# A second level of Strassen's algorithm for the first two weight products of eight token blocks, with weight forms kept in HBM

## The chip, the cores and the metric

The kernel runs on one core of a Trainium2 chip. Its engines are TensorE (PE, with its weight loads shown apart as PEld), VectorE (DVE), ScalarE (ACT), GpSimd (POOL) and SyncE (SP), which issues DMAs; ACT issues some DMAs too. The metric is device time in microseconds of one execution, as the median of several.

## The reference

```python
# attention, float32: 8 batches, 8 heads, 576 positions, head size 64
scores = (1.0 / np.sqrt(64)) * np.matmul(q, k.transpose(0, 1, 3, 2))
gamma = 1.0 - 2.0 ** (-5.0 - np.arange(8))
Dmat = np.where(rel >= 0, gamma[:, None, None] ** rel[None], 0.0)   # rel = i - j
attn_out = np.matmul(scores * Dmat[None], v)
# feed forward over 8*576 = 4608 tokens of width 512
x = attn_out.transpose(0, 2, 1, 3).reshape(4608, 512)
a = x @ w1            # 512 -> 1024
b = x @ w2            # 512 -> 1024
out = ((a * b) @ w3) @ w_out     # 1024 -> 1024 -> 512
```

q, k and v come as float32, the four weights as float64.

## The kernel before

**Start.** The weights are read as float64 and converted to float32 on the chip. w3 and w_out are multiplied with each other once (`w3_mm`, L499) into `w3o`, 1024x512, so that each token afterwards needs only two products: `x` with w1 and w2, and `a*b` with `w3o`. This is mixed with the first pair of batches.

**Attention.** Batches are taken in four pairs. The 576 positions of a pair are cut into five chunks of 64, 128, 128, 128 and 128 positions, which gives 20 chunk steps `g`. In one step `pv(g)` multiplies masked scores with v and the running state (L296, L321) and ACT copies the result into `xT` (L328), token columns of x; then `state(g + 1)` (L277) and `score(g + 1)` (L255) run for the next chunk. From chunk 7 on (`in_blocks`), q and k are brought in by `load_blocks` (L182, DMAs at L193): 32 DMAs of 32 KB on SP's queue for a chunk of 128 positions, 16 for one of 64, into two buffers of the tag `ld_q`, one for q and one for k. DVE transposes them out of these buffers (`front_blocks`, L212), after POOL has scaled q (`scale_blocks`, L203). POOL also scales v (L226). v, and k in token order, are loaded on ACT's queue.

**Feed forward.** The tokens of a pair are cut into three blocks of 192 positions by two batches, twelve blocks `m` in all. `up(i, n, fp)` (L529) computes one quarter of the columns of a and b for one block by Strassen's algorithm: the depth is halved, and the two batches of the block are the two columns of the token matrix. It has seven products of four matmuls of 128x128 by 128x192 (L546), a float32 matmul standing as two records in the trace. The weight operands are prepared once, in place, in two tiles `wA` (A11, A12, S3, A22) and two tiles `wS` (S1, S2, S4), one of each per half of the 1024 columns (`strassen_weights`, L171). The token operands of a block are prepared by POOL (`strassen_tokens`, L518). ACT and DVE move the products out of PSUM: ACT copies at L559 and L574, DVE adds at L551 (`plus`), and DVE multiplies the a part with the b part into `ab` at the end (L580). PSUM's pool `acc` holds seven buffers.

`down` (L645) takes two tiles of 128 tokens of `ab` and multiplies them with `w3o` (L661), again by Strassen: seven products of four matmuls by 128x256, added by DVE (L665) into the tile `ot`, which has one buffer, and stored on ACT's queue (L709). Its token operands (L627, L631, L633) are formed by DVE beforehand: `ahead` puts them on the list `aside`, from which each `plus` of an `up` takes one. `carry` (L611) copies the third tile of tokens of an even block away, so that it can be paired with that of the next block.

**Order.** All engines run in the order in which the program issues to them. `todo` lists the calls of `up`, `carry` and `down` that are ready, and `work(n)` does the next `n` of them. In chunk step `g` the order is: n - 1 pieces of work; one more piece, among whose additions DVE's two transposes for chunk g + 1 are put (through `aside`); the loads of chunk g + 2 on SP (`load_blocks`); then `pv(g)`, loads of v and k on ACT's queue, `state` and `score` of g + 1, and the scaling on POOL. `n` is the length of `todo` divided by the chunk steps left in the pair. After the last chunk of a pair `add_pair` adds the pair's work to `todo`.

Of the kernel before, what the change touches and what calls it, by code (L numbers as in the profile page):

```python
# [12 lines left out]
BF16 = mybir.dt.bfloat16  # L13
ALU = mybir.AluOpType
PSUM = bass.MemoryType.PSUM

@with_exitstack
def kernel(
# [13 lines left out]
    nc = tc.nc  # L57
# [448 lines left out]
    def has_x(i, n):  # L506
        return any(starts[c] + sizes[c] >= (n + 1) * TB and ("x", i * NC + c) in live for c in range(NC))
# [21 lines left out]
    def up(i, n, fp, conv=0, tail=True, first=False):  # L529
        m = every.index((i, n))  # L530
        while ("S", fp) not in live:
            assert go_on() is None
        if ("B", i, n) not in live:
            list(strassen_tokens(i, n))
        if fp == 0:
            live["ab", i, n] = (pools["ab3"] if m == 2 else ffn).tile([P, 2 * KF, TB], F32, tag="ab", name="ab")
        ab = live["ab", i, n]

        def product(ps, a, b):
            a, b = A(fp, a), live["B", i, n][b]  # L540
            new = ps is None
            if new:
                ps = acc.tile([P, 2, TB], F32, tag="acc", name="up")
            for w in range(2):
                for r in range(2):
                    nc.tensor.matmul(ps[:, w, :], a[:, w, r, :], b[:, r, :], start=(new and w == r == 0),  # L546
                                     stop=(w == r == 1), skip_group_check=True)
            return ps

        def plus(ps, to, sb):  # L550
            nc.vector.tensor_add(c[:, to], ps, c[:, sb])  # L551
            convert(conv.pop(0) if isinstance(conv, list) else conv)
            if aside:
                aside.pop(0)()


        c = ffn.tile([P, 4, 2, TB], F32, tag="c", name="c", bufs=1)
        p1 = product(None, "A11", "B11")
        nc.scalar.copy(c[:, 0], p1)  # L559

        convert(owed.pop() if owed else 0)
        if first:

            p7 = product(None, "S3", "T3")
            product(p1, "A12", "B21")
            aside.pop(0)()
        plus(product(None, "S2", "T2"), 1, 0)
        plus(p7 if first else product(None, "S3", "T3"), 2, 1)
        p5 = product(None, "S1", "T1")
        plus(p5, 3, 2)  # L570
        plus(product(None, "A22", "-T4"), 2, 2)
        if not first:
            product(p1, "A12", "B21")
        nc.scalar.copy(c[:, 0], p1)  # L574
        product(p5, "S4", "B22")
        plus(p5, 1, 1)

        if fp == NQ - 1 and m + 1 < len(every) and has_x(*every[m + 1]) and ("B", *every[m + 1]) not in live:
            list(strassen_tokens(*every[m + 1]))
        nc.vector.tensor_mul(ab[:, 4 * fp:4 * fp + 4, :], c[:, :, 0, :], c[:, :, 1, :])  # L580
        if tail:
            convert(conv)

    aside, owed = [], []

    def w3_sums():

# [53 lines left out]
            aside.append(todo_sums.pop(0))  # L643

    def down(x, y, then=None, last=False):  # L645
        for m, t in (x, y):
            if t == 2 and m % 2 == 0 and m > 0:
                assert (m, t) in carried
        a, done, left = pair_of(x, y)
        ahead(x, y)  # L650
        while len(done) < 3:
# [11 lines left out]

        def plus(nm, to, sb):
            nc.vector.tensor_add(ot[:, to[0], to[1]], ps[nm], ot[:, sb[0], sb[1]])  # L665

        def put(m, t, row, half=slice(0, 2)):

# [176 lines left out]
    load_blocks(NC + 1, "q")  # L845
    keep_stores.clear()
    store()
    todo = [(down, (0, 0), (0, 1)), (down, (1, 0), (1, 1)), (down, (0, 2), (1, 2))]

    def add_pair(i):  # L850

        for n in range(NB):
            m = every.index((i, n))
            if m != NB:
                todo.append((up, i, n, 1))
            if m > NB and m % 2 == 0:
                todo.append((down, (m - 2, 2), (m - 1, 2)))
            if m != NB:
                todo.extend((up, i, n, fp) for fp in range(2, NQ))
            if m + 1 < len(every):  # L860
                todo.append((up, *every[m + 1], 0))
                if m % 2 == 0:
                    todo.append((carry, m, 2))
            else:
                todo.append((down, (m - 1, 2), (m, 2)))
            todo.append((down, (m, 0), (m, 1)))

    def work(n):
        for _ in range(min(n, len(todo))):
            fn, *args = todo.pop(0)  # L870

            nxt = next((x for x in todo if x[0] is not carry), None)
            if nxt and nxt[0] is down and fn is not carry:
                if fn is down:
                    args.append(nxt[1:])
                else:
                    last = args == [*every[max(nxt[1][0], nxt[2][0])], NQ - 1]
                    ahead(*nxt[1:], 1 if last else 3)
            if g == G and not todo:
                fn(*args, last=True)  # L880
            else:
                fn(*args)

    g = NC
    scale_blocks(NC)
# [4 lines left out]
    score(NC)  # L890
    scale_blocks(NC + 1)
    in_blocks = [u >= 2 * NC - 3 for u in range(G)] + [False] * 2
    for g in range(NC, G):
        c = g % NC

        n = (1, 1, 2, 2, 1)[c] if g < 2 * NC else -(-len(todo) // (NC - c))
        if g + 2 < G and not in_blocks[g + 2]:
            load(g + 2, "k")
            load_blocks(g + 2, "q")
        if g + 1 < G:  # L900
            scale(g + 1, "v")
            if not in_blocks[g + 1]:
                front(g + 1, "k")
                front_blocks(g + 1, "q")
        half = (n + 1) // 2
        if in_blocks[g + 1]:
            scale_blocks(g + 1)

            work(n - 1)
            aside.extend(lambda nm=nm: front_blocks(g + 1, nm) for nm in "kq")  # L910
            work(1)
            while aside:
                aside.pop(0)()
            half = 0
        if in_blocks[g + 2]:
            load_blocks(g + 2, "q")
            load_blocks(g + 2, "k")
        work(half)
        pv(g)()

        if g + 2 < G:
            queue = nc.scalar if in_blocks[g + 2] else nc.sync
            load(g + 2, "v", queue)
            if in_blocks[g + 2] and (g + 2) % NC != NC - 1:
                load(g + 2, "k", queue)
        if g + 1 < G:
            state(g + 1)
            score(g + 1)
        if g + 2 < G and not in_blocks[g + 2]:
            scale_blocks(g + 2)  # L930
        if g == NC + 1:
            list(strassen_tokens(1, 0))
            todo.extend((up, 1, 0, fp) for fp in range(NQ))
        if not (in_blocks[g + 1] and g + 1 < G):
            work(n // 2)
        if c == NC - 1:
            add_pair(g // NC)
    g = G
    work(len(todo))

# [42 lines left out]
```

## Time and profile before

| what | value |
|---|---|
| runs | 856.2, 856.49 and 858.15 us |
| median | 856.49 us |
| span of the profiled execution | 853.3 us |
| mean granted TensorE clock in it | 0.996 |
| moved by DMA | 64.52 MB, 76 GB/s over the span |
| ACT copies of an `up` (128x384) | 479 ns at L559, 476 at L574 |
| DVE multiplication at the end of an `up` (128x768) | 983 ns |
| POOL scaling of v (128x1024) | 1963 ns |

The span is what the profiler saw from the first to the last instruction; the runs are timed apart, and their median is 3.2 us above it. The profile's busy time of an engine is a sum over instructions, so an engine that is busy 98% of the span has few gaps, while one that is busy 55% may still be the last to arrive at some place. A group line gives the program line, the engine, the operation, the tile written and those read, the shape, the count, the busy time and mean duration, and then the idle time of the engine ahead of these instructions with what ended it. A name with q (SPq) is the time for which an engine's instruction queue was held at that place, by issuing or by waiting.

### The profile page before, as it was taken

The numbers are of one execution on the slowest core, as the hardware profiler recorded it, in microseconds if no ns is written. First come the engines' busy times: TensorE is split into PE (matmuls) and PEld (weight loads), VectorE is DVE, ScalarE is ACT, GpSimd is POOL, SyncE is SP. The second block draws the span as 40 slices with busy tenths as digits, with TensorE's granted clock in tenths as the row PEclk, the third lists the DMA queues.
The fourth block names the chain that finished last, engine by engine and source line by source line (L and its number), as shares of the span: only waits on it lengthen the run. The fifth ranks groups of instructions, "written<-read, shape, count | busy, mean of one in ns | idle before, by whom it ended". The sixth has DMA issues, their size and how long they took to land.

```text
span 853.3 us, 15401 instructions
## 1 busy us (share of the span) xinstructions
PE 839.5 (98%) x6273; PEld 766.0 (90%) x6273; DVE 469.8 (55%) x763; ACT 205.7 (24%) x385; POOL 111.0 (13%) x95
## 2 busy tenths in 40 slices
PE   7999999999999999999999999999999999999998
PEld 6889999644888999999999999999999999999996
DVE  4999999990744454454545444544454434334343
ACT  4777566670111102011111010110100201001000
POOL 1100010002104113130230130203030101000000
PEclk8999999999999999999999999999999999999999
DMA  9994554526057446252452161542130000000001
GB/s 193 223 228 113 77 151 121 142 80 111 12 107 122 83 69 107 53 101 45 79 97 46 24 108 36 90 82 43 38 62 26 2 25 1 25 26 1 25 1 49
DMA packets 220485, 64.52 MB, mean 76 GB/s; under 512 B 201336, under 2 KB 211832, under 8 KB 220416
## 3 DMA queue, kind: packets, MB, share of 16 engines
q1 hardware_dynamic: 169856, 42.80, 26.1%
q10 hardware_dynamic: 50560, 20.75, 10.9%
q8 instruction: 49, 0.80, 0.4%
q14 instruction: 20, 0.16, 0.1%
HBM read 54.08 MB, written 9.44 MB: 74 GB/s over the span
## 4 chain that ended last, share of the span: by engine, by line
PE 88%; DVE 6%; DMA 3%; issue 2%; ACT 1%; SPq 0%; POOL 0%; ACTq 0%; DVEq 0%; POOLq 0%
PE up L546 46%; PE po L661 25%; PE ps L499 6%; PE xps L321 4%; PE sc L255 4%; DMA ld_v<-in_v_dram 2%; PE xps L296 2%; PE st L277 2%; DVE c L551 1%; DVE m L424 1%; PE tp L240 1%; DVE wS L171 1%; DVE e L435 1%; DMA out_dram<-ot 1%; DMA raw<-in_moe_w_out_dram 0%
## 5 line engine op out<-in xcount | busy, mean ns | idle before, releaser
L551 DVE TENSOR_TENSOR c<-up,c 128x384 f32<-128x384 f32 x240 | 132.5, 552 | 180.0 <-PE up L546 176.2
L546 PE MATMUL up<-xT,wA 128*128 128x192 f32 x1152 | 212.0, 327 | 0.0
L546 PEld LDWEIGHTS up<-xT,wA 128*128 128x128 f32 x1152 | 190.6, 190 | 2.8 <-issue 0.5
L546 PE MATMUL up<-T,wS 128*128 128x192 f32 x768 | 140.4, 326 | 0.9 <-DVE wS L171 0.9
L546 PEld LDWEIGHTS up<-T,wS 128*128 128x128 f32 x768 | 127.4, 190 | 1.1 <-ACT c L559 1.1
L661 PE MATMUL po<-w3o,ab 128*128 128x256 f32 x456 | 104.3, 380 | 0.6 <-DVE ab L627 0.3
L661 PEld LDWEIGHTS po<-w3o,ab 128*128 128x128 f32 x456 | 85.9, 190 | 12.8 <-DVE ab L627 0.7
L665 DVE TENSOR_TENSOR ot<-po,ot 128x256 f32<-128x256 f32 x90 | 38.1, 423 | 71.6 <-PE po L661 68.3
L574 ACT COPY c<-up 128x384 f32<-128x384 f32 x48 | 22.9, 476 | 218.8 <-PE up L546 212.8
L226 POOL TENSOR_TENSOR ld_v<-ld_v,gk 128x1024 f32<-128x1024 f32 (+1 forms) x18 | 35.3, 1963 | 298.9 <-DMA ld_v<-in_v_dram 214.5
L546 PE MATMUL up<-xT,wS 128*128 128x192 f32 x384 | 70.9, 328 | 1.6 <-DVE c L551 1.6
L546 PE MATMUL up<-T,wA 128*128 128x192 f32 x384 | 70.2, 326 | 0.0
L258 DVE TENSOR_TENSOR pm<-sc,mask 128x512 f32<-128x512 f32 (+1 forms) x80 | 45.4, 628 | 41.0 <-PE sc L255 41.0
L546 PEld LDWEIGHTS up<-xT,wS 128*128 128x128 f32 x384 | 63.4, 190 | 2.9 <-DVE c L551 2.7
L661 PE MATMUL po<-wB,forms 128*128 128x256 f32 x288 | 65.1, 379 | 0.0
L546 PEld LDWEIGHTS up<-T,wA 128*128 128x128 f32 x384 | 63.7, 190 | 0.0
L661 PEld LDWEIGHTS po<-wB,forms 128*128 128x128 f32 x288 | 54.7, 190 | 7.4
L499 PE MATMUL ps<-wo,w3T 128*128 128x512 f32 x128 | 55.1, 592 | 0.0
L559 ACT COPY c<-up 128x384 f32<-128x384 f32 x48 | 23.0, 479 | 132.1 <-PE up L546 77.4
L499 PEld LDWEIGHTS ps<-wo,w3T 128*128 128x128 f32 x128 | 24.3, 190 | 30.1 <-issue 29.7
L580 DVE TENSOR_TENSOR ab<-c 128x768 f32<-128x768 f32 x48 | 47.2, 983 | 4.3 <-ACT c L574 0.6
L203 POOL TENSOR_TENSOR bl_q<-bl_q,gqs 128x512 f32<-128x512 f32 (+1 forms) x30 | 32.4, 1100 | 100.3 <-DMA bl_q<-in_q_dram 92.5
(80 smaller groups left out, 797.6 us busy)
## 6 DMA issues: line engine op xcount, KB each, us to landing
raw<-in_moe_w_dram SPq DMA_DIRECT2D x72, 128.0 KB, 3.0
bl_q<-in_q_dram SPq DMA_DIRECT2D x216, 32.0 KB, 2.2
bl_k<-in_k_dram SPq DMA_DIRECT2D x192, 32.0 KB, 2.1
out_dram<-ot ACTq DMA_DIRECT2D x23, 256.0 KB, 2.0
ld_v<-in_v_dram ACTq DMA_DIRECT2D x11, 512.0 KB, 5.9
raw<-in_moe_w_dram SPq DMA_DIRECT2D x16, 256.0 KB, 6.2
raw<-in_moe_w_out_dram SPq DMA_DIRECT2D x32, 128.0 KB, 2.8
ld_k<-in_k_dram ACTq DMA_DIRECT2D x8, 512.0 KB, 8.3
```

The costliest lines, as they stand in the source:

```text
L203: nc.gpsimd.tensor_tensor(out=part, in0=part, in1=gqs[:, :, n0:n0 + n].unsqueeze(3).to_broadcast([P, NP, n, BL]), op=ALU.mult)
L226: engine.tensor_tensor(out=t, in0=t, in1=gam[:sz, c].unsqueeze(1).unsqueeze(3).to_broadcast([sz, 2, H, D]), op=ALU.mult)
L255: nc.tensor.matmul(sc[j][:sz, p, :sz], kT[hs, b, p, :sz], qT[hs, b, p, :sz], start=True, stop=True)
L258: nc.vector.tensor_mul(pm[:sz, b, j, :, :sz], sc[j][:sz, :, :sz], mask[:sz, :sz].unsqueeze(1).to_broadcast([sz, NP, sz]))
L321: nc.tensor.matmul(banks[r][heads[half], b, n, :sz], vs[:sz, b * H + 2 * p + j, :], pm[:sz, b, j, p, :sz], start=(c == 0 and m == 0), stop ...
L499: nc.tensor.matmul(ps, live["w3T", ft][:, g, :], live["wo"][:, g, :], start=(g == 0), stop=(g == KF - 1))
L546: nc.tensor.matmul(ps[:, w, :], a[:, w, r, :], b[:, r, :], start=(new and w == r == 0), stop=(w == r == 1), skip_group_check=True)
L551: nc.vector.tensor_add(c[:, to], ps, c[:, sb])
L559: nc.scalar.copy(c[:, 0], p1)
L580: nc.vector.tensor_mul(ab[:, 4 * fp:4 * fp + 4, :], c[:, :, 0, :], c[:, :, 1, :])
L661: nc.tensor.matmul(ps[nm], a[A][:, f, :], live["W"][B][:, f, :], start=(f == 0 and not on), stop=(f == NP - 1), skip_group_check=True)
L665: nc.vector.tensor_add(ot[:, to[0], to[1]], ps[nm], ot[:, sb[0], sb[1]])
```

## The change

Blocks 0 to 3 are computed as before. Blocks 4 to 11 are taken in four groups of two, and `up` is replaced there by `up2`, which applies Strassen's algorithm twice. The two blocks of a group are the two token columns of the outer level; the inner level is the former one.

**Steps.** For a group and a half of the 1024 columns the outer level has seven operands (P1, P2, P6, P7, P4, P5, P3 in this order), and each is one step, a call of `up2`: seven products of two matmuls by 128x192 each. There are 4 groups x 2 halves x 7 = 56 steps in place of 8 x 4 = 32 calls of `up`. The results of the steps are added among each other by POOL (`combine`, on tiles of 128x768 elements), from four tiles `cc`, and DVE multiplies a with b for each finished quarter (`multiply`).

**Weight forms.** Each half has seven outer operands, each with seven inner ones. They are computed on DVE in place (`weight_forms`), by two sets of additions per half, and each set is followed by DMAs on SP (14 per set, 28 per half) that store what it has finished in HBM tiles `kept`. One operand is 128 x 1792 elements, 917,504 bytes. These pieces are put on a list `spread`, from which `plus` of `up` and `plus` of `down` take one each. Afterwards `wA` is used again as a ring of three slots for operands read back (`open_second`), and `wS` as the `cc` tiles. `next_forms` issues the read of one operand on SP, in the step after the slot's last use, for the step two later.

**Token forms.** `token_forms` makes both levels of token operands for a group by 19 operations on POOL, at the end of the chunk step in which the group's tokens are complete.

**Order.** `n` comes from a written list, `dealt`. The downs of a group follow its 14 steps, one after the other. In the last chunk step all `n` pieces come ahead of `pv`. `carry` is used for block 2 alone. The down (1, 0), (1, 1) and that of (2, 2), (3, 2) move behind the `up`s of block 3 = (1, 0), in whose additions the weight forms are computed.

```diff
             convert(conv.pop(0) if isinstance(conv, list) else conv)
-            if aside:
-                aside.pop(0)()
+            for extra in (aside, spread):
+                if extra:
+                    extra.pop(0)()
...
-    todo = [(down, (0, 0), (0, 1)), (down, (1, 0), (1, 1)), (down, (0, 2), (1, 2))]
-
-    def add_pair(i):
-
-        for n in range(NB):
-            m = every.index((i, n))
-            if m != NB:
-                todo.append((up, i, n, 1))
-            if m > NB and m % 2 == 0:
-                todo.append((down, (m - 2, 2), (m - 1, 2)))
-            if m != NB:
-                todo.extend((up, i, n, fp) for fp in range(2, NQ))
-            if m + 1 < len(every):
-                todo.append((up, *every[m + 1], 0))
-                if m % 2 == 0:
-                    todo.append((carry, m, 2))
-            else:
-                todo.append((down, (m - 1, 2), (m, 2)))
-            todo.append((down, (m, 0), (m, 1)))
+    todo = [(down, (0, 0), (0, 1)), (down, (0, 2), (1, 2))]
...
+    FORM = 14 * P
+    OPERANDS = {"P1": ("A11", "B11"), "P2": ("A12", "B21"), "P6": ("S2", "T2"), "P7": ("S3", "T3"),
+                "P4": ("A22", "-T4"), "P5": ("S1", "T1"), "P3": ("S4", "B22")}
+    PLACE = {"A11": (0, 0), "A12": (1, 0), "S3": (0, 1), "A22": (1, 1)}
+    hbm = ctx.enter_context(tc.tile_pool(name="hbm", bufs=1, space=DRAM))
+    kept = {(h, nm): hbm.tile([P, FORM], F32, tag=f"kept{h}{nm}", name="kept")
+            for h in halves for nm in (*PLACE, "S1", "S2", "S4")}
...
+    def weight_forms(h, second):
+
+        wa, ws = wA[h].rearrange("p r j c n -> p (r j) c n"), wS[h]
+
+        def tt(out, in0, in1, op):
+            def both():
+                for w in (wa, ws):
+                    o, x, y = (w[:, :, c, m * QC:(m + 1) * QC] if w is wa else w[:, :, m, :, c, :]
+                               for m, c in (out, in0, in1))
+                    nc.vector.tensor_tensor(out=o, in0=x, in1=y, op=op)
+            return both
+
+        def send(pieces):
+            for nm in (*PLACE, "S1", "S2", "S4"):
+                to = kept[h, nm]
+                for lo, m, c in pieces:
+                    n = 2 * P if c == 1 else 4 * P
+                    d = to[:, lo:lo + n].rearrange("p (g n) -> p g n", n=P)
+                    cs = slice(0, 2) if c is None else slice(c, c + 1)
+                    if nm in PLACE:
+                        r, f = PLACE[nm]
+                        x = wA[h][:, r, :, cs, m * QC + f * P:m * QC + f * P + P]
+                    else:
+                        x = wS[h][:, ("S1", "S2", "S4").index(nm), m, :, cs, :]
+                    nc.sync.dma_start(d.rearrange("p (j c) n -> p j c n", j=2), x)
+
+        if second:
+            return [tt((1, 1), (1, 1), (1, 0), ALU.subtract), tt((0, 0), (1, 1), (0, 0), ALU.add),
+                    tt((0, 1), (0, 1), (1, 1), ALU.subtract),
+                    lambda: send([(8 * P, 0, None), (12 * P, 1, 1)])]
+        return [tt((1, 0), (0, 0), (1, 0), ALU.subtract), lambda: send([(0, 0, None), (4 * P, 1, None)])]
...
+    order = ("P1", "P2", "P6", "P7", "P4", "P5", "P3")
+    ring, sent, steps, free = [], [0], [0], []
+    groups = [(m, m + 1) for m in range(4, len(every), 2)]
...
+    def open_second():
+        while spread:
+            spread.pop(0)()
+        ra = [wp.tile([P, 32 * P], F32, tag=f"wA{h}", name="ra") for h in halves]
+        cs = [wp.tile([P, 2, 4, 2, TB], F32, tag=f"wS{h}", name="cc") for h in halves]
+        ring.extend([ra[0][:, :FORM], ra[0][:, FORM:2 * FORM], ra[1][:, :FORM]])
+        free.extend(cs[h][:, j] for h in halves for j in range(2))
+        live["T2"] = ra[1][:, FORM:].rearrange("p (s k c t) -> p s k c t", s=2, k=3, c=2)
...
+        for _ in range(2):
+            next_forms()
+        live["U"] = [ffn.tile([P, 2, TB], F32, tag="T", name="u", bufs=5) for _ in range(5)]
...
+    def next_forms():
+        n = sent[0]
+        if n < 14 * len(groups):
+            nc.sync.dma_start(ring[n % 3], kept[n % 14 // 7, OPERANDS[order[n % 7]][0]])
+            sent[0] += 1
...
+    def multiply():
+        while results:
+            gr, h, f, b, z, used = results.pop(0)
+            for s, m in enumerate(groups[gr]):
+                if ("ab", *every[m]) not in live:
+                    live["ab", *every[m]] = ffn.tile([P, 2 * KF, TB], F32, tag="ab", name="ab")
+                ab = live["ab", *every[m]].rearrange("p (q i) t -> p q i t", i=4)[:, 2 * h:2 * h + 2, 2 * f + b, :]
+                v = z.rearrange("p (m s) w t -> p m s w t", s=2)[:, :, s]
+                nc.vector.tensor_mul(ab, v[:, :, 0, :], v[:, :, 1, :])
+            free.append(z)
...
+    def up2(gr, n):
+
+        h, key = n // 7, order[n % 7]
+        slot = ring[steps[0] % 3]
+        B = live["B2", gr][OPERANDS[key][1]]
+        steps[0] += 1
+        c = free.pop(0)
+        sums2[key] = c
...
+        adds = {"P1": [], "P2": [("P2", "P1")], "P6": [("P6", "P1")], "P7": [("P7", "P6")], "P4": [("P4", "P7")],
+                "P5": [("P7", "P5"), ("P6", "P5")], "P3": [("P3", "P6")]}[key]
...
+            for w in range(2):
+                nc.tensor.matmul(ps[:, w, :], weight_of(slot, a, w), B[b], start=(new and w == 0), stop=True,
+                                 skip_group_check=True)
...
+        def combine(part):
+            for into, of in adds:
+                o, i = sums2[into][:, part], sums2[of][:, part]
+                nc.gpsimd.tensor_tensor(out=o, in0=o, in1=i, op=ALU.add)
+
+        p1 = product(None, "A11", "B11")
+        nc.scalar.copy(c[:, 0], p1)
+        finish()
+        next_forms()
+        plus(product(None, "S2", "T2"), 1, 0)
+        plus(product(None, "S3", "T3"), 2, 1)
+        p5 = product(None, "S1", "T1")
+        plus(p5, 3, 2)
+        plus(product(None, "A22", "-T4"), 2, 2)
+        combine(slice(2, 4))
+        multiply()
+        product(p1, "A12", "B21")
+        nc.scalar.copy(c[:, 0], p1)
+
+        def rest():
+            product(p5, "S4", "B22")
+            plus(p5, 1, 1)
...
+    real = (up, up2, down)
+
+    def add_group(gr):
+        X, Y = groups[gr]
+        todo.extend((up2, gr, n) for n in range(14))
+        todo.extend([(close_up2,), (down, (X, 0), (X, 1)), (down, (X, 2), (Y, 2)), (down, (Y, 0), (Y, 1))])
...
-            nxt = next((x for x in todo if x[0] is not carry), None)
-            if nxt and nxt[0] is down and fn is not carry:
+            nxt = next((x for x in todo if x[0] in real), None)
+            if nxt and nxt[0] is down:
                 if fn is down:
                     args.append(nxt[1:])
                 else:
-                    last = args == [*every[max(nxt[1][0], nxt[2][0])], NQ - 1]
-                    ahead(*nxt[1:], 1 if last else 3)
+                    ahead(*nxt[1:], 1 if fn is up2 else 3)
             if g == G and not todo:
                 fn(*args, last=True)
             else:
                 fn(*args)
+            n -= 1
+            while todo and todo[0][0] not in real:
+                todo.pop(0)[0]()
...
+    dealt = [1, 1, 2, 2, 2, 3, 4, 4, 4, 3, 7, 7, 3, 7, 7]
     for g in range(NC, G):
         c = g % NC
-
-        n = (1, 1, 2, 2, 1)[c] if g < 2 * NC else -(-len(todo) // (NC - c))
+        n = dealt[g - NC]
...
+            forms = [(lambda h=h, second=second: spread.extend(weight_forms(h, second)),)
+                     for h in halves for second in (False, True)]
+            ups = [(up, 1, 0, fp) for fp in range(NQ)]
+            todo.extend([*ups[:2], forms[0], ups[2], forms[1], ups[3], forms[2], (down, (1, 0), (1, 1)), forms[3],
+                         (down, (2, 2), (3, 2)), (open_second,), (down, (3, 0), (3, 1))])
...
+        if not (in_blocks[g + 1] and g + 1 < G) and half:
             work(n // 2)
-        if c == NC - 1:
-            add_pair(g // NC)
+        if g == 2 * NC - 1:
+            add_group(0)
+        ready = {2 * NC - 1: 0, 2 * NC + 3: 1, 3 * NC + 1: 2, G - 1: 3}
+        if g in ready:
+            token_forms(ready[g])
+            if ready[g]:
+                add_group(ready[g])
```

The other functions are `open_second`'s further tiles, the body of `token_forms` (additions and subtractions on POOL between views of `xT`, `T2`, `E` and `U`), and `weight_of`, which picks one 128x128 weight tile out of a slot.

## The prediction

> **What bounds the kernel now.** I read the page's busy table and slices, then the chain of waits in order of time, then the SP queue's timeline, since the change puts 56 large loads there.
>
> ```profile
> PE 839.5 (98%) x6273; PEld 766.0 (90%) x6273; DVE 469.8 (55%) x763; ACT 205.7 (24%) x385; POOL 111.0 (13%) x95
> ...
> PE 88%; DVE 6%; DMA 3%; issue 2%; ACT 1%; SPq 0%; POOL 0%; ACTq 0%; DVEq 0%; POOLq 0%
> ```
>
> PE is the bound. In the chain (start, length, what; x counts instruction records) the second half is PE work end to end:
>
> ```profile
> 402.23 1.03 PE xps L296 x32
> 403.26 1.90 PE xps L321 x32
> 405.16 0.93 PE st L277 x32
> 406.09 1.99 PE sc L255 x32
> ...
> 688.55 36.40 PE up L546 x224
> 724.95 12.09 PE po L661 x56
> ```
>
> Four `up` take 36.40, so one is 9.10 us, 56 records of 0.1625; a `down` is 12.09; the attention of a chunk is 5.85. The SP queue (start, length, instruction, count), the waits of its blocked loads, and the transposes that wait for those:
>
> ```profile
> 266.19 11.42 SPq L193 DMA_DIRECT2D bl_q<-in_q_dram  x16
> 277.72 9.39 SPq L193 DMA_DIRECT2D bl_k<-in_k_dram  x16
> 327.28 8.58 SPq L193 DMA_DIRECT2D bl_q<-in_q_dram  x16
> 335.97 11.80 SPq L193 DMA_DIRECT2D bl_k<-in_k_dram  x16
> ...
> SPq L193 <- DVE kT L212: 129.9, 12, 27.3
> ...
> 288.82 1.25 DVE L212 STREAM_TRANSPOSE kT<-bl_k 128x1024 f32<-128x1024 f32 x1 [1.14 <-DMA bl_k<-in_k_dram]
> ```
>
> The 32 loads of a full chunk hold SP for 20.4 us; they can start only when DVE has transposed the previous chunk's tiles out of the same buffers. Today nothing urgent stands behind them.
>
> Prices from elsewhere. The groups of a DVE and a POOL addition (count, busy, mean ns, idle before):
>
> ```profile
> L551 DVE TENSOR_TENSOR c<-up,c 128x384 f32<-128x384 f32 x240 | 132.5, 552 | 180.0 <-PE up L546 176.2
> ...
> L518 POOL TENSOR_TENSOR T<-xT,T 128x384 f32<-128x384 f32 x20 | 21.0, 1057 | 163.8 <-PE up L546 163.1
> ```
>
> Two windows after PE had starved (PE, PEld, DVE, ACT, POOL busy, granted clock, DMA share, GB/s):
>
> ```profile
> 12.00:16.00 4.00, 3.49 (x64) 3.49 (x64) 2.62 (x5) 1.86 (x4) 0.46 (x1) 0.50 1.35 221
> 16.00:20.00 4.00, 3.29 (x21) 3.02 (x18) 2.55 (x4) 2.78 (x6) 0.00 (x0) 0.67 1.15 263
> ```
>
> The packets of a queue that only stores, 640 to 853 (packets, MB, share of 16 engines):
>
> ```profile
> q10 hardware_dynamic: 2224, 3.67, 5.4%
> ```
>
> and of the loads' queue, 300 to 500:
>
> ```profile
> q1 hardware_dynamic: 52566, 6.35, 21.3%
> ```
>
> **What the Trainium skill says.** "DMA: Bandwidth & Descriptors", Issuing engines are not separate DMA queues: starting a DMA costs its sequencer time that is "usually small relative to the DMA itself". Here it is not small: a 32 KB load lands in 2.1 us, but 32 of them occupy SP for 20.4. Same page, Anatomy of one DMA: about 2 us fixed plus bytes over bandwidth, and a wait before a DMA is held on the issuing sequencer; the trace agrees (256 KB stores land in 2.0). "TensorE: Matmul & The Clock Gate", Part 1: after about 3.4 us of idleness PE runs at half clock until busy again; the trace shows 0.50 and 0.67 after a starved stretch, worth (0.50 + 0.33) x 4 = 3.3 us. "GPSIMD Engine Reference", section 3.1: a two-input add costs about twice VectorE's; the trace has 1057 against 552.
>
> **The matmuls.** Removed: 32 `up` x 9.10 = 291.2. Added: 56 steps of 14 matmuls, 28 records, x 0.1625 = 4.55 each, 254.8. Gain 36.4, the ceiling. Downs stay at 18.
>
> **The refills, the main cost.** A step reads 917,504 B of weights from a ring of three. Its refill is issued on SP one step after its slot was left, two steps ahead. In the changed program's order six refills stand behind a chunk's 32 blocked loads; these are the third steps of work in chunk steps 11, 12, 13, 15, 16, 18. Call the last step before such a boundary T = 0. Its third product ends at 1.95, DVE adds (0.55), transposes k (1.24), adds, transposes q: 5.8. SP then issues 32 loads, to 26.2; the refill issues and lands. Landing isn't in the trace: 2.0 for a 256 KB store is the floor; the store packets' 83 ns for 1650 B (5.4% of 16 engines x 213 us over 2224) are 318 GB/s, so 2.0 + 2.1 for the further 655 KB, with issue about 4.9; 31.1. PE meanwhile: 4.55 + 5.85 + two resident steps 9.1 = 19.5. It waits 11.6. Entering 15 and 18 the transposes come at a down's end (q done 1.3 after PE), so 1.3 + 20.4 + 4.9 = 26.6 against 14.2 and 15.0: 12.4 and 11.6. Entering 11, POOL works through 19 token forms first (8 x 1.06 + 4 x 1.9 + smaller = 22.7), and `scale_blocks`, hence the q transpose, stand behind them: 19. Sum 11.6 x 3 + 12.4 + 11.6 + 19 = 78. Afterwards SP catches up within a stretch: 5 us per refill against two steps of lead.
>
> **Keeping the forms.** DVE sums per half are 4 x (128x1024 + 128x768), 1.2 + 1.0 = 2.2 each. The second set overwrites columns that the first set's 14 stores still read, so DVE waits for these, in front of PE's releases. Third `up` of block (1, 0) starts at 300, fourth at 309; before that the second waits 3.6 for its k tiles (they land at 289 as now, the work comes earlier). SP is busy with loads until 292 + 20.4 = 313. 3.67 MB in 512 B packets: 7168 packets over 16 engines, at 31 ns interpolated between 13 (121 B, q1 above) and 83 ns: 13.9, + 2, so 329; DVE's remaining work 5, PE waits from 317 to 333: 16. The second half repeats it in the down of (2, 2), (3, 2): 6, and ACT's loads of v and k there share semaphores with these stores, so its copies hold a down by 3. The token forms of the first group reuse wA of half 1, so POOL starts when the last stores landed (386), reaches T2 12 us later, PE wants it at 391, and T1 and -T4 after: 9. Sum 3.6 + 16 + 6 + 3 + 9 = 38, bounds 15 (stores drain at 20 ns, little waits) and 55.
>
> **The rest.** POOL's 112 sums of 768: extrapolating 1057 for 384, 1.9 each, 14 in 7 steps, 26.6 of 31.9 us: they run late by about a step around P5 and P3, which seven PSUM banks cover, except at the end of the last group: 3. Three downs now follow each other in each group: `ot` has one buffer, and the one such place now stalls PE 0.3, x 8 = 2.4. DVE per step 5 x 0.55 + multiplies 0.6 = 3.4 of 4.55: hidden. Nine waits over 3.4 us cost clock: 0 to 3.3 each, I take 1: 9.
>
> **Sum.** 853.3 - 36.4 + 78 + 38 + 5.4 + 9 = 947.3. The profile's span lies 3.2 below the median of 856.49: 950.5, I say 951.
>
> **Rivals.**
> - Refills late, stores free. For: DMA is idle half the time at 290 to 320 and stores might drain fast. Against: the second set names the same columns. 853.3 - 36.4 + 78 + 5.4 + 6 + 3.2 = 909.
> - Faster: refills come in time and the gain survives. It is decided at SP: 32 loads would have to pass in 8.8 us (20.4 - 11.6), 0.28 each; the shortest issue in the trace is 0.31, the median 0.45. It needs some 16 of the loads to be out earlier. Then 853.3 - 36.4 + 5.4 + 5 of DVE sums + 3.2 = 830.
> - The ring is bound by bandwidth: 0.918 MB per 4.55 us is 202 GB/s, and the page's best slice moved 228 with small packets. Then each of 56 steps would take 5.1 at 180 GB/s, + 31, and loads add more: 985 to 1010. Against: those slices were packets under 512 B.
>
> **How the numbers follow.** Forecast 0.60 (925 to 985), stores free 0.19 (890 to 925), bandwidth 0.09 (over 985), faster 0.10, no change 0.02. Range 895 to 1000, 8 in 10 or a little more. 0.3% is what a measurement of this kernel tells from no change: faster 0.10, same 0.02, slower 0.88.
>
> **What would show it.** Right: a wait of PE `up` on `ra<-kept` with six long entries near 11 us each; SP's 20 us of loads just ahead of those refills; DVE waiting on `kept` DMA twice; steps of 4.55 in the last group without gaps; PEclk dips after 310. Wrong: those refills issued within some 15 us of the last step, SP loads shorter than now, or gaps spread evenly over steps (bandwidth), or in DVE behind POOL's `cc` sums.

## The result, and the profile after

The changed kernel takes 977.94 us (median of 4 runs, 977.65 to 980.26), the one before 856.69 (4 runs). The ratio is 1.1415, with a 95% interval from 1.1395 to 1.1434. The prediction was 951, in a range from 895 to 1000.

The page of the changed kernel, with the busy times, the slices of PE and of its clock, and the shares of the chain that ended last:

```profile
PE 848.6 (87%) x6049; PEld 759.6 (78%) x6049; DVE 614.8 (63%) x931; ACT 224.6 (23%) x429; POOL 378.1 (39%) x251
...
PE   9999999999999579649768895958896998898988
...
PEclk9999999999999898879788997978997999999999
...
PE 54%; DVE 15%; DMA 14%; SPq 9%; issue 5%; ACT 1%; POOL 0%; DVEq 0%; ACTq 0%; POOLq 0%
```

PE is still the busiest engine, but only 54% of the chain is now PE's. The rest of it runs through DVE, DMA and SP's queue, which had 6%, 3% and nothing. The slices of PE are full up to about a third of the span, which is where the weight forms begin, and the clock dips in the same slices.

Both kernels reach the same `pv`, the last before the `up`s of block (1, 0), after some 267 us (266.2 before, 267.5 after). The second part can therefore be compared as a whole. The answer of the windows has start and end, length, then the busy times of PE, PEld, DVE, ACT and POOL with their instruction counts, the granted clock, the DMA share and GB/s. First the kernel before:

```profile
266.20:849.60 583.40, 583.13 (x4425) 552.18 (x4424) 268.74 (x428) 69.88 (x150) 87.57 (x72) 1.00 0.27 52
```

then the changed one:

```profile
267.60:972.60 705.00, 587.98 (x4201) 542.05 (x4200) 413.01 (x596) 88.62 (x194) 354.77 (x228) 0.92 0.49 134
```

PE was idle for 0.3 us before and is idle for 117.0 now. Its busy time went up by 4.9 us, although 36.4 us of matmuls went away (from the prices of the prediction). So the same matmuls took 41.3 us longer, at a clock of 0.92 instead of 1.00. The sum is -36.4 + 116.7 + 41.3 = 121.6, which is the difference of the two stretches; the other 1.3 us by which the spans differ lie ahead of them.

113.4 of the 117.0 us of idle time are 23 gaps of more than 0.6 us. Each gap's first instruction names what released it. Here are some of them in the timeline of PE, where the brackets have the idle time and the releaser:

```profile
328.11 2.93 PE L523 MATMUL up<-xT,wS 128*128 128x192 f32 x8 [8.61 <-DVE c L528]
...
409.88 3.79 PE L232 MATMUL sc<-qT,kT 64*128 64x128 f32 x32 [7.11 <-DVE qT L189]
...
435.50 1.62 PE L969 MATMUL up<-ra 128*128 128x192 f32 x4 [12.54 <-DMA ra<-kept]
...
505.80 2.90 PE L969 MATMUL up<-ra 128*128 128x192 f32 x8 [7.88 <-DMA ra<-kept]
...
549.54 3.23 PE L636 MATMUL po<-w3o,ab 128*128 128x256 f32 x8 [4.46 <-ACT ot L660]
...
677.02 1.65 PE L969 MATMUL up<-xT,ra 128*128 128x192 f32 x4 [4.33 <-DVE cc L974]
```

Added up by cause, and set against the prediction's terms:

| part | predicted, us | in the profile, us |
|---|---|---|
| matmuls removed less added | -36.4 | -36.4 (prices of before) |
| refills and loads of chunks (six waits on `ra<-kept` 51.1; score 7.1; ACT behind POOL 5.1 and behind loads 1.7) | 78 | 65.0 |
| weight forms and their stores (2.4 + 8.6 + 4.4 + 1.2) | 38 | 16.6 |
| DVE late at the end of a half or a group, five gaps behind `cc` | 3 | 15.6 |
| downs that follow each other (4.5 + 2.9 + 4.7 + 2.6, forms 1.5) | 2.4 | 16.2 |
| slower clock | 9 | 41.3 |
| gaps under 0.6 us | 0 | 3.6 |

The two terms that the prediction made most of were too large by 34 us together, and the three small ones below them were too small by 59.

### The profile page after: what moved, and what is told of

The parts are those of the page before. It is cut to its first block, busy times and chain, and to the rows that moved or that the text cites. A ratio compares the mean times of both kernels' runs of the same rounds, so it can differ in the third digit from the quotient of the medians.

```text
span 976.2 us, 15738 instructions
## 1 busy us (share of the span) xinstructions
PE 848.6 (87%) x6049; PEld 759.6 (78%) x6049; DVE 614.8 (63%) x931; ACT 224.6 (23%) x429; POOL 378.1 (39%) x251
## 4 chain that ended last, share of the span: by engine, by line
PE 54%; DVE 15%; DMA 14%; SPq 9%; issue 5%; ACT 1%; POOL 0%; DVEq 0%; ACTq 0%; POOLq 0%
PE up L969 16%; PE po L636 14%; PE up L523 9%; SPq L170 7%; PE ps L476 6%; DMA ld_k<-in_k_dram 4%; DVE cc L974 4%; DMA ra<-kept 3%; DVE ab L949 3%; PE xps L298 2%; PE sc L232 2%; DMA out_dram<-ot 2%; DMA bl_q<-in_q_dram 2%; DMA kept<-wS 2%; SPq L861 2%
## 5 line engine op out<-in xcount | busy, mean ns | idle before, releaser
L981 POOL TENSOR_TENSOR cc<-cc 128x768 f32<-128x768 f32 x112 | 209.6, 1887 | 141.8 <-DVE cc L974 140.6
L974 DVE TENSOR_TENSOR cc<-up,cc 128x384 f32<-128x384 f32 x280 | 153.8, 554 | 101.8 <-PE up L969 80.2
L969 PE MATMUL up<-xT,ra 128*128 128x192 f32 x512 | 110.1, 345 | 27.1 <-DVE cc L974 17.0
L969 PE MATMUL up<-ra 128*128 128x192 f32 x384 | 82.4, 347 | 47.9 <-DMA ra<-kept 47.9
L969 PEld LDWEIGHTS up<-xT,ra 128*128 128x128 f32 x512 | 90.2, 200 | 32.4 <-DVE cc L974 23.3
L949 DVE TENSOR_TENSOR ab<-cc 128x384 f32<-128x384 f32 x64 | 81.6, 1315 | 31.5 <-POOL cc L981 31.5
L969 PE MATMUL up<-e,ra 128*128 128x192 f32 x384 | 73.1, 327 | 0.0
L523 PE MATMUL up<-xT,wA 128*128 128x192 f32 x384 | 70.6, 328 | 0.0
L528 DVE TENSOR_TENSOR c<-up,c 128x384 f32<-128x384 f32 x80 | 44.0, 550 | 36.8 <-PE up L523 36.3
L523 PEld LDWEIGHTS up<-xT,wA 128*128 128x128 f32 x384 | 63.3, 190 | 1.3 <-issue 0.7
```

What stands on the lines that cost most here:

```text
L949: nc.vector.tensor_mul(ab, v[:, :, 0, :], v[:, :, 1, :])
L969: nc.tensor.matmul(ps[:, w, :], weight_of(slot, a, w), B[b], start=(new and w == 0), stop=True, skip_group_check=True)
L981: nc.gpsimd.tensor_tensor(out=o, in0=o, in1=i, op=ALU.add)
```

## The experiments

Unless something else is said, each changes only what its diff shows in the changed kernel. The time of the kernel before was 856.5 to 856.8 in the three series.

### Refills on another queue

```diff
-            nc.sync.dma_start(ring[n % 3], kept[n % 14 // 7, OPERANDS[order[n % 7]][0]])
+            nc.scalar.dma_start(ring[n % 3], kept[n % 14 // 7, OPERANDS[order[n % 7]][0]])
```

> Only the queue of the 56 refills changes, from SP's to ACT's, where no block loads stand ahead of them. Theory (the refills are late because 32 loads and their waits stand ahead of them on SP): the six waits of PE on ra<-kept, 51.1 us together, fall below 5, the dips of the clock behind them (some 2 us each) go too, 978 - 51 - 12 = about 915 us. Rival (the reads themselves are slow: 917,504 bytes per step against loads and stores on the same DMA engines): the waits stay over 25 us in sum and the time over 945.

What it is about is seen in the changed kernel. First SP's timeline around the longest wait:

```profile
408.17 14.41 SPq L170 DMA_DIRECT2D bl_q<-in_q_dram  x16
422.68 7.79 SPq L170 DMA_DIRECT2D bl_k<-in_k_dram  x16
430.57 14.04 SPq L896 DMA_DIRECT2D ra<-kept  x4
```

The 32 loads hold SP for 22.2 us, and the first refill is issued at 430.57. The first matmul that reads it runs at 435.50, 4.9 us later; the prediction had 20.4 and 4.9. The reads were not held up by the memory.

Measured: 953.69 us (ratio 1.1127, 1.1091 to 1.1163). The waits on `ra<-kept` are gone from the gaps except for two of 0.7 us, so the theory is right about the refills. But the time fell by 24 us, not by 63. A gap of 11.9 us now stands one product behind the place where the one of 12.5 stood, with another releaser, DVE. POOL's timeline of this run shows why (start, length, instruction, idle time and releaser):

```profile
413.14 1.90 POOL L203 TENSOR_TENSOR ld_v<-ld_v,gk 128x1024 f32<-128x1024 f32 x1 [1.26 <-DMA ld_v<-in_v_dram]
425.31 2.06 POOL L180 TENSOR_TENSOR bl_q<-bl_q,gqs 128x512 f32<-128x512 f32 x2 [10.26 <-DMA bl_k<-in_k_dram]
427.33 3.56 POOL L981 TENSOR_TENSOR cc<-cc 128x768 f32<-128x768 f32 x2
```

and DVE's:

```profile
429.16 2.61 DVE L949 TENSOR_TENSOR ab<-cc 128x384 f32<-128x384 f32 x2 [12.34 <-POOL cc L981]
431.69 2.99 DVE L974 TENSOR_TENSOR cc<-up,cc 128x384 f32<-128x384 f32 x5
```

POOL comes to the scaling of the next chunk's q, waits 10.3 us for the loads, and the additions `cc` stand behind it. DVE's multiplication waits for these additions, and DVE's own additions, which would free PSUM for PE, wait behind the multiplication. The same 22 us of loads thus reach PE by a second way, hidden until then by the first.

The edit also has a cost of its own. In front of a down PE now waits 7.7 us for a copy of ACT, which comes behind ACT's refills and its loads of v and k (issued at 382.0 and 383.2, in the changed kernel at 375.2 and 377.4); the changed kernel has no gap there. What held ACT at these loads was not tested.

### The scaling of q behind the work

```diff
-            scale_blocks(g + 1)
-
             work(n - 1)
+            scale_blocks(g + 1)
             aside.extend(lambda nm=nm: front_blocks(g + 1, nm) for nm in "kq")
```

It is made on top of the refills on ACT's queue.

> The refills on ACT's queue as in the run before, and in addition POOL's scaling of the next chunk's q moves behind the first n - 1 pieces of work of a chunk step, just ahead of DVE's transposes. Theory (with the refills in time, the 20 us of loads still hold PE, now through POOL: the scaling waits for the loads, POOL's additions wait behind it, DVE's multiplication for these and PE for DVE): the gaps of 11.9, 8.3 and 7.2 us behind DVE or ACT cc fall to 4 us or less each, what is left being loads against 24 us of PE work per chunk step; 954 - 16 - 5 = about 933 us. Rival (the loads bind through DVE's transposes as well, wherever POOL stands): the same gaps stand in front of the score or in front of DVE's additions after the transposes, time over 948.

Measured: 932.04 us (1.0891, 1.0846 to 1.0937), 21.7 less than with the refills alone. The gap of 11.9 is gone; at that place PE now waits 1.6 us for the refill and, at the end of the chunk step, 4.9 us in front of the score for DVE's transposes. The rival has a share too: at the end of the first group's steps, where the changed kernel waits 4.3 us, PE now waits 7.5 us for DVE's additions, which stand behind a transpose that waits 4.6 us for the loads. The gap behind ACT that came with the refills is 10.2 us here. The two edits together take 46 us off, so the block loads on SP cost about that or more, with the clock behind their waits. Some of it is still there, since 24 us of PE work in a chunk step do not cover 22 us of loads, the scaling and the transposes.

### Without the sums of the second set

```diff
-            return [tt((1, 1), (1, 1), (1, 0), ALU.subtract), tt((0, 0), (1, 1), (0, 0), ALU.add),
-                    tt((0, 1), (0, 1), (1, 1), ALU.subtract),
-                    lambda: send([(8 * P, 0, None), (12 * P, 1, 1)])]
+            return [lambda: send([(8 * P, 0, None), (12 * P, 1, 1)])]
```

> Leaves out the three sums of the second set of weight forms in each half (12 DVE additions), so the stored forms are not the right ones; all stores and refills stay. Theory (these sums wait for the first set's stores, and PE waits for DVE behind them): the gaps of 8.61 and 4.43 us at the fourth quarter of block (1, 0) and in the down of (2, 2), (3, 2) go, with their clock dips 978 - 13 - 4 = about 961 us; SP then stores the second set earlier and the token forms of the first group start earlier, which may bring another 5. Rival (PE waits there for something else, the k tiles or the stores of ot): gaps of 4 us or more stay at both places, time over 970.

Measured: 964.29 us (1.1229, 1.1166 to 1.1292). The gaps of 8.61 and 4.42 us are gone. In their place PE, which comes to the first step earlier, waits there 2.4 us for the first refill and 4.5 for POOL's token forms. The edit takes away the sums' own time together with their wait, so it doesn't separate the two. It agrees with the theory, and with DVE's timeline of the changed kernel, where the second set begins with two waits for stores:

```profile
319.07 1.23 DVE L846 TENSOR_TENSOR wA<-wA 128x1024 f32<-128x1024 f32 x1 [2.95 <-DMA kept<-wA]
323.04 0.96 DVE L846 TENSOR_TENSOR wS<-wS 128x768 f32<-128x768 f32 x1 [2.74 <-DMA kept<-wS]
323.91 0.55 DVE L528 TENSOR_TENSOR c<-up,c 128x384 f32<-128x384 f32 x1
```

The last store that DVE needs has landed by 323.0. The prediction had 329, from packets of 31 ns and an end of the loads at 313; SP began the stores at 311.3. PE began to wait at 319.5 instead of 317 and went on at 328.1 instead of 333, so 16 us of stall became 8.6.

### The sets apart

```diff
-            todo.extend([*ups[:2], forms[0], ups[2], forms[1], ups[3], forms[2], (down, (1, 0), (1, 1)), forms[3],
+            todo.extend([*ups[:2], forms[0], *ups[2:], forms[2], forms[1], (down, (1, 0), (1, 1)), forms[3],
```

> Only the place of the weight forms changes: the second set of the first half moves from the fourth quarter of block (1, 0) into the down behind it, after the first set of the second half. Theory (the second set came before the first set's stores had landed): the gap of 8.61 us goes and no gap over 3 us comes in its place in the next two downs but for one of 3 to 5 in front of the last, 978 - 9 - 2 = about 967 us. Rival (it is DVE's own work of 26 us that PE waits for, wherever it stands): the gap moves into the downs, time over 974.

Measured: 968.0 us (1.1291, 1.1262 to 1.132). The 8.6 us are gone, and the downs behind have gaps of 1.3, 3.8, 1.0 and 4.5 us instead of 1.2, 2.6 and 4.4. Ahead of the one of 3.8, ACT has been idle for 12.8 us, until stores of `wS` landed; the one of 4.5, in the down ahead of the steps, is behind ACT as well, whose copy follows its load of k (issued at 368.1). Both theories have a share, the first the larger one: moving the sums away from the stores took off 10 us with the clock.

### Without the additions of the results

```diff
-            for into, of in adds:
+            for into, of in ():
```

This leaves out all 112 additions on POOL.

> Leaves out the 112 additions among the steps' results on POOL. Theory (POOL's sums run late at P5 and P3, and while POOL works a DVE operation with both inputs in SBUF takes 2.1 instead of 0.5 us, so that DVE's additions come late): the multiplication's mean falls from 1.31 to 0.5 us, the five gaps of PE behind DVE cc (15.6 us) and the one of 5.1 behind ACT go, 978 - 21 - 8 = about 949 us. Rival (DVE is simply full): the multiplication stays above 1 us and the gaps stay, time over 970.

Measured: 950.95 us (1.1108, 1.1071 to 1.1144). The group of DVE's multiplications, in the changed kernel (count, then busy, mean ns, and idle time before with its releaser):

```profile
L949 DVE TENSOR_TENSOR ab<-cc 128x384 f32<-128x384 f32 x64 | 81.6, 1315 | 31.5 <-POOL cc L981 31.5
```

and without POOL's additions:

```profile
L949 DVE TENSOR_TENSOR ab<-cc 128x384 f32<-128x384 f32 x64 | 37.2, 622 | 0.0
```

The same instruction on tiles of the same shape takes less than half as long. DVE's additions `cc<-up,cc`, which read one operand from PSUM, took 554 ns in the one and 555 in the other. In the timeline of the changed kernel's last group both cases stand next to each other:

```profile
896.27 4.24 DVE L949 TENSOR_TENSOR ab<-cc 128x384 f32<-128x384 f32 x2 [0.56 <-POOL cc L981]
900.43 3.00 DVE L974 TENSOR_TENSOR cc<-up,cc 128x384 f32<-128x384 f32 x5
903.35 1.02 DVE L949 TENSOR_TENSOR ab<-cc 128x384 f32<-128x384 f32 x2
```

Two multiplications take 4.24 us while POOL adds (four additions from 892.34 to 900.09) and 1.02 where POOL is idle. The Trainium skill states this in "GPSIMD Engine Reference", section 1, Specifications: GpSimd's interfaces to SBUF are shared with VectorE, and an instruction of VectorE with two SBUF inputs contends with it. The trace agrees, and gives the price here: 2.1 us instead of 0.5. POOL pays less: the four additions beside these multiplications took 1.81 to 2.12 us, the shortest of all 112 took 1.80.

Of the five gaps behind DVE `cc`, three of 2.1 to 2.7 us are gone, and two of 4.3 became 2.0. The gaps fell by only 13 us in sum, because the refills came later against a faster PE (59.6 us of waits instead of 51.1). What the slower clock costs fell too, from 41.3 to 28.2.

### The last addition of a down first

```diff
-        while aside:
-            aside.pop(0)()
         plus(3, C12, C12)
+        while aside:
+            aside.pop(0)()
```

> In a down the last addition into ot moves ahead of the sums for the next down, which DVE otherwise does first. Theory (in three places these sums run beside POOL's token forms, take 2.2 instead of 0.7 us each and so hold up the addition, the store and the next down's first copy): PE's gaps of 4.46, 2.94 and 4.74 us in front of a second down fall below 1, 978 - 11 - 4 = about 963 us. Rival (the store's own landing of 2.0 us and the single buffer are the whole wait): gaps of 2 us and more stay, time over 972.

Measured: 966.83 us (1.127, 1.1219 to 1.1321). DVE in the changed kernel, at the end of a group's first down:

```profile
540.29 2.27 DVE L605 TENSOR_TENSOR ab<-ab 128x512 f32<-128x512 f32 x1
542.60 2.19 DVE L609 TENSOR_TENSOR forms<-ab 128x512 f32<-128x512 f32 x1
544.82 1.77 DVE L611 TENSOR_TENSOR forms<-forms,ab 128x512 f32<-128x512 f32 x1
546.51 0.41 DVE L640 TENSOR_TENSOR ot<-po,ot 128x256 f32<-128x256 f32 x1
```

and with the addition first:

```profile
544.42 0.42 DVE L640 TENSOR_TENSOR ot<-po,ot 128x256 f32<-128x256 f32 x1 [1.30 <-PE po L636]
544.76 2.27 DVE L605 TENSOR_TENSOR ab<-ab 128x512 f32<-128x512 f32 x1
```

The three sums for the next down have two SBUF inputs each and run beside POOL's token forms, so they take 6.2 us; in the downs at 350 us two of them took 0.69 each. In the downs of the last group, where POOL is idle, all three take 0.7 each in the same order of work, and PE waits 0.3 us at that place. In front they held the last addition, its store, and through the one buffer `ot` the next down's first copy. With the order turned, the three gaps of 4.46, 2.94 and 4.74 are gone, with one of 1.1 in their place. What looked like a wait for the one buffer `ot` was mostly this contention.

### The edits together

Refills on ACT's queue, scaling behind the work, sets apart, the addition first, and `dealt` with 4 instead of 3 pieces in chunk step 10 and 2 instead of 3 in step 14.

> Refills on ACT's queue, scaling behind the work, sets apart, the last addition of a down first, and one piece of work moved from chunk step 14 to 10. If the causes add up: 933 - 11 - 15 - 3 = about 904 us, with some 45 us of gaps and a clock of 0.965. If they hide each other (one wait in place of the next): over 920.

Measured: 902.2 us (1.0533, 1.0474 to 1.0593). Taken one by one, the refills with the scaling take 45.9 us off, the sets apart 9.9 and the addition first 11.1, which would give 911. So the causes do not hide each other. The other 9 us are not assigned, since the pieces moved by `dealt` were not run alone. In the second part PE is idle for 55.2 us instead of 117.0 (same columns as above):

```profile
270.10:899.10 629.00, 573.84 (x4201) 531.44 (x4200) 409.48 (x597) 88.25 (x194) 357.56 (x228) 0.96 0.57 150
```

Then 16 of POOL's additions given to DVE:

```diff
-                nc.gpsimd.tensor_tensor(out=o, in0=o, in1=i, op=ALU.add)
+                (nc.vector if into == "P6" and of == "P5" else nc.gpsimd).tensor_tensor(out=o, in0=o, in1=i, op=ALU.add)
```

> As the one before, and DVE instead of POOL adds P5's results to P6's (16 of the 112 additions). Theory (POOL falls behind by a step at P5 and P3): the gaps behind DVE cc at the end of a half fall by half, some 8 us with their clock dips less than the kernel before it. Rival (DVE, not POOL, is what comes late): the gaps grow by 2 us a half, 8 us more.

Measured: 913.36 us (1.0666, 1.0641 to 1.0692), 11 us more. The rival holds: DVE comes late, and moving work from POOL to it makes that worse (the 16 additions take DVE 1.44 us each). The gaps at the ends of the halves are 4.3, 6.5, 4.3, 1.7 and 4.3 us, where they were 2.1, 4.6, 2.1, 2.7 and 2.1.

The longest gap left in the five edits together, 9.2 us in front of a down, was behind ACT: its copy of the state waited for stores of weight forms. So the loads of v and k of that chunk step went to POOL's queue:

```diff
-            queue = nc.scalar if in_blocks[g + 2] else nc.sync
+            queue = nc.gpsimd if g == 2 * NC - 1 else nc.scalar if in_blocks[g + 2] else nc.sync
```

> The five edits together, and in chunk step 9 alone the loads of v and k go to POOL's queue instead of ACT's. Theory (ACT is held there by these loads, which wait for stores of weight forms, and a down waits 9.2 us for ACT's first copy): this gap falls below 2 us, 902 - 8 - 2 = about 892 us. Rival (the copy itself waits for the stores, or POOL's token forms then start as much later): the gap stays or comes back in front of the first step that needs the token forms, time over 898.

Measured: 909.72 us (1.0627, 1.0609 to 1.0644). The rival holds. The gap left that place and came back as one of 11.5 us at the second product of the first step. POOL's timeline:

```profile
363.36 1.30 POOL L905 TENSOR_TENSOR xT<-xT 128x384 f32<-128x384 f32 x1
376.09 0.99 POOL L905 TENSOR_TENSOR ra<-xT 128x384 f32<-128x384 f32 x1 [11.43 <-DMA kept<-wS]
```

The token forms take the place of the weights in the ring's tile, and so wait until the last stores of weight forms have landed, at 376. In the version before it these token forms began at 372.2, and ACT's wait covered most of the wait for them; here they also begin 3.9 us later. This is the prediction's term of 9 us for the first token forms; in the changed kernel PE came late enough for it not to show, and where the second sums were left out it showed with 4.5. The second part of this version is 6.8 us longer than that of the five edits (2.2 of idle time, 4.6 of slower matmuls), the medians differ by 7.5; the runs of the five edits spread from 898.8 to 908.4.

Last, the same kernel without POOL's additions:

> The kernel before it in this call, without the 112 additions on POOL (so the result leaves these sums out): a bound for everything that another distribution of the sums could bring. If the sums and their contention with DVE are the larger part of what is left over (about 40 us of gaps and 25 of clock): under 870 us. If loads, forms and stores are: over 880. In neither case should it come under the 856 of the kernel before by more than the measurement can tell.

Its second part, in the same columns:

```profile
267.20:873.60 606.40, 563.53 (x4201) 526.51 (x4200) 364.25 (x597) 88.06 (x194) 147.03 (x118) 0.97 0.58 155
```

Measured: 880.55 us (1.0283, 1.0261 to 1.0304). The additions, with what they do to DVE and to the clock, are worth 29 us in this version, a third of the 89 us that it lies above the ceiling of some 820 (856.7 - 36.4). Without them it is still 24 us slower than the kernel before. That lies at the limit of 880 set for loads, forms and stores as the larger part (the runs go from 878.9 to 882.3), and well over the 870 for the sums. What remains are 40 us of gaps of more than 0.6 us: one of 11.6 for the token forms, three of 3.7 to 4.4 for the loads, and smaller ones at the downs and the weight forms. No version that computes everything came closer to the kernel before than 45 us. Fewer and larger block loads, or room for the token forms outside the ring's tile, were not run, so whether the second level can win here stays open.

## Why the prediction came out as it did

- **Direction and range** were right, and so was the picture: six waits on `ra<-kept`, the longest of 12.5 us, each behind 17 to 22 us of loads; DVE waiting twice for `kept`; the clock dipping after 310.
- **The matmuls.** The ceiling of 36.4 stands: the last group's steps run at 4.55 us with gaps only at the ends of its halves, and leaving waits away moved the time toward it by as much as was left away.
- **The refills**, 78, came to 65.0. The first entry, 19, is 7.1 in front of the score and 12.5 at the refill, 19.6. The following five were put at 11.6 to 12.4 each and measured 8.2 (5.1 behind POOL, 3.1 at the refill), 7.9, 10.2, 10.0 and 7.4. The mechanism is as described, only the size is off. What the prediction did not see is the second way of the same loads, through POOL's scaling; without the experiment on the queue all of it would have been put down to the refills.
- **Keeping the forms**, 38, came to 16.6. The terms: 3.6 became 2.4, 16 became 8.6, 6 + 3 became 4.4 + 1.2, because the stores drained sooner than taken. The 9 us for the first token forms did not show. The term is real, as the last versions have it with 11.5, but PE's other waits covered it.
- **The rest** is where the prediction failed, in terms that hid the error of the first two: 34 us too much there and 59 too little here cancel in part, so that the sum came within 27 us of the measured time is partly luck. "DVE per step 5 x 0.55 + multiplies 0.6 = 3.4 of 4.55: hidden" took the multiplication at the duration that it has alone. Beside POOL it takes 2.1 us, so DVE is late at the ends of halves (15.6 us instead of 3) and the sums of the downs too (16.2 instead of 2.4). POOL is busy for 39% of the span now, for 13% before. The trace of the kernel before shows the effect all the same, in its few places with POOL at work. Of the 18 sums at L627, the 13 beside an idle POOL took at most 0.68 us; at 340 us, beside POOL's scaling of v and q, one took 2.21:

```profile
340.49 2.21 DVE L627 TENSOR_TENSOR ab<-ab 128x512 f32<-128x512 f32 x1
364.87 0.67 DVE L627 TENSOR_TENSOR ab<-carry,ab 128x512 f32<-128x512 f32 x1
340.26 1.90 POOL L226 TENSOR_TENSOR ld_v<-ld_v,gk 128x1024 f32<-128x1024 f32 x1 [7.88 <-DMA ld_v<-in_v_dram]
342.12 2.96 POOL L203 TENSOR_TENSOR bl_q<-bl_q,gqs 128x512 f32<-128x512 f32 x2
```

A mean over a group hides it. "GPSIMD Engine Reference" of the Trainium skill, which the prediction used for POOL's price, states it too, in the section named above.
- **The rivals.** That the ring is bound by bandwidth fell: the late refill landed 4.9 us after its issue, and issued in time the refills kept no wait over 4 us in any version. That the refills come in time and the gain survives, 830, was wrong twice: the refills came late, and with them in time the kernel takes 954.
- **The clock**, "nine waits over 3.4 us", at 1 us each, was a loss of 41.3 us. Both factors are wrong. There are 13 waits over 3.4 us, and behind each of them the clock dips; but it also dips behind some of the seven from 2.1 to 3.2 us. Behind the longest (windows as above):

```profile
423.00:435.50 12.50, 0.00 (x0) 0.03 (x1) 5.21 (x7) 0.48 (x1) 9.04 (x6) 0.67 0.59 153
435.50:439.50 4.00, 4.00 (x13) 4.00 (x14) 0.56 (x1) 0.48 (x1) 0.47 (x2) 0.50 0.39 134
439.50:443.50 4.00, 4.00 (x22) 4.00 (x21) 2.23 (x4) 0.48 (x1) 1.92 (x2) 0.82 0.59 217
443.50:447.50 4.00, 4.00 (x29) 3.77 (x30) 3.21 (x4) 0.48 (x1) 3.17 (x2) 1.00 0.53 177
```

The four microseconds behind the gap run at 0.50 and the next four at 0.82, a loss of 2.0 + 0.7 = 2.7. The prediction had worked out 3.3 for such a place and taken 1. Behind the short waits the length does not decide. After two of 2.12 us each the windows are:

```profile
814.30:818.30 4.00, 3.97 (x69) 3.40 (x70) 3.92 (x3) 0.29 (x1) 3.71 (x2) 1.00 0.50 150
931.90:935.90 4.00, 4.00 (x12) 3.34 (x13) 3.99 (x4) 0.00 (x0) 3.62 (x2) 0.57 0.00 0
```

Over the kernels the loss goes more closely with the number of waits of more than 2 us than with the idle time:

| kernel | waits over 2 us | idle time of PE, us | longer matmuls, us | per wait |
|---|---|---|---|---|
| changed | 20 | 117.0 | 41.3 | 2.1 |
| without the additions | 16 | 102.2 | 28.2 | 1.8 |
| five edits | 12 | 55.2 | 27.1 | 2.3 |
| and loads of v, k on POOL | 13 | 57.4 | 31.7 | 2.4 |
| and without the additions | 9 | 42.9 | 16.8 | 1.9 |

In the six other kernels, added up in the same way, a wait goes with 2.2 to 2.6 us.

## What to carry to other kernels

When a transfer is late behind a busy queue, look for every other consumer of what keeps that queue busy: moving the transfer alone may only change the name of the wait. Price an element-wise operation beside the neighbour that it will have, not from a stage where that neighbour is idle; the longest of a group shows what its mean hides. Where PE begins to wait, count the waits and charge those over 2 us with some two microseconds of slower matmuls each on top of their length, as an average; in this kernel that was over a quarter of what was lost (41 of 158 us).

## What the hardware showed that was not expected

- A DVE operation on 128x384 with both inputs in SBUF took 0.5 us alone and up to 2.2 us while POOL worked (means 622 and 1315 ns without and with POOL's additions). POOL lost less: an addition of 128x768 took 1.80 us at the shortest, 1.89 in the mean and 2.25 at the most. DVE operations with one input in PSUM lost nothing (554 and 555 ns).
- A refill of 896 KB held ACT's queue for 0.33 us (median with the five edits), less than one load of 32 KB held SP's (14.41 us for 16), and landed 4.8 us after its issue (4.6 from SP's queue in the changed kernel). So it isn't the bytes that hold a queue; whether it is the number of DMAs or that of their pieces (128 bytes each in the loads) was not separated.
- In five kernels with the same PE work the granted clock in the second part was 0.92, 0.94, 0.95, 0.96 and 0.97 at 20, 16, 13, 12 and 9 waits of more than 2 us. Every one of the 13 waits over 3.4 us in the changed kernel was followed by a dip; waits of 2.1 us were followed by one in some places and by none in others.
